# Attention's value matmuls in groups of three key chunks, newest chunk first

## The chip, the cores and the metric

The kernel runs on one core of one Trainium2 chip. The metric is the device time of one execution in microseconds (us); lower is better. Engines are named as in the profile: PE is TensorE's matmul side and PEld its weight loads, DVE is VectorE, ACT is ScalarE, POOL is GpSimd, SP is SyncE, which issues the DMAs.

## The reference

Three parts follow each other: an attention whose queries are pooled by two, and two mixture-of-experts layers on its output.

```python
def _attn_ref(q, k, v):            # each (4, 8, 1152, 64), float32
    B, H, S, D = q.shape
    q_pool = q.reshape(B, H, S // 2, 2, D).mean(axis=3)
    scores = (1.0 / np.sqrt(D)) * np.matmul(q_pool, k.transpose(0, 1, 3, 2))
    scores = scores - np.max(scores, axis=-1, keepdims=True)
    attn = np.exp(scores)
    attn = attn / (np.sum(attn, axis=-1, keepdims=True) + 1e-09)
    return np.matmul(attn, v)

def reference(...):
    x = attention output as (B * 576, H * 64) = (2304, 512)
    x = moe(x, w_gate, w1, w2)     # 8 experts, each takes its best 288 tokens
    return moe2(x, w_skip, w_gate, w1, w2)
```

The change touches the last line of the attention alone. The two expert layers take the second half of the time and are the same before and after.

## The kernel before, in words

Attention works on 16 **pairs**: one batch entry and two neighbouring heads (j = 0, 1). A pair has 9 chunks of 128 keys and two halves of 288 queries (h = 0, 1), so 18 **score steps** (h, c). For one step, `scores` (L213) issues four matmuls on PE: two of 128x128 with 288 columns in float16 (L224, tile `st`), and two of 65x128 (L226), which add the low parts of the split numbers and the negative row maximum. ACT then takes the exponential of both heads at once into a float32 tile `E` (L228), and POOL adds the tile up over the chunks (L233, L235; in the last pair DVE does). `av` (L237) multiplies the chunk's 128 keys of `E` with the values `vt` (L242): one call for each head j, into partitions 0 to 63 or 64 to 127 of the same PSUM tile `av`. A float32 call is two matmuls and two loads in the trace, so a chunk is four matmul rows of 128*64 ("x4"), and one head's half of it is "x2". After the ninth chunk ACT copies `av` out as `o` (L246). `norm` (L249) sums `es` over the partitions with two float32 matmuls of the same 64 columns (L253, tile `ms`), and DVE takes the reciprocal (L256) and multiplies (L257).

While PE works on a pair, it prepares a later one. `scales` (L124 and L129 on ACT and PE, L132 to L145 on DVE) finds power-of-two scales; `split_k` (L151 on ACT, L152 on DVE), `split_q` (L163) and `split_ql` (L167) split into float16 parts; SP transposes them by DMA (L174, L182). `mx` (L193, L196, L197) computes 27 score blocks of 384 keys into the rotating tiles `ms`, whose row maxima DVE reduces (L198); `mxrow` (L205, L207) reduces those nine by nine and transposes them for L226. The pool of `ms` has three buffers, which `mx`, `norm`, `scales`, `tokmajor` (L267, transposes of the finished output) and `logits`/`fold` (L287, L300) share. `st` has two buffers, `E` six, `av` one, `vt` two.

What orders the work: every piece is entered in a plan with a due time in units of score steps (`TA`, `TA0`, `TAL`; a pair is `NSL` = 18 steps) and the plan is emitted sorted by due time. SP keeps the emitted order. For PE, DVE, ACT and POOL a scheduler then goes by emitted order, but passes over what it does not expect to be ready, so the written order is a priority only. Each engine runs its own list strictly in order. The value matmuls of step n are due at n + 3.63:

```python
at(T, (0, 1.0), [lambda i=i, h=h, c=c: scores(i, h, c) for h, c in order])
at(T, (TA["av"], 1.0), [lambda i=i, h=h, c=c: av(i, h, c) for h, c in order])
```

Of the kernel before, what the change touches and what calls it, by code (L numbers as in the profile page):

```python
# [14 lines left out]
P = 128  # L15
NSL = 18
TA = dict(load=-48.62, loadv=-18.39, A=[-35.94, -35.47, -31.75, -29.03, -30.29, -28.09, -23.67], mx=(-19.82, 0.54),
          row=-5.54, av=3.63, norm=[12.26, 21.29], log=[20.27, 23.07, 28.12, 38.2], out=[32.31, 31.08])
TA0 = dict(load=[-94.38, -66.16, -35.31], loadv=[-45.83, -22.29], A=[-76.98, -72.14, -71.71, -68.33, -69.55, -69.2,
          -65.64], mx=(-66.05, 1.19), mx2=(-27.49, 0.55), A1=[-62.02, -58.75, -50.59, -41.02, -44.45, -46.24, -43.53])  # L20
TAL = dict(log=[21.4, 21.59, 24.82, 32.89])
# [26 lines left out]
def attention(tc, q, k, v, w_gate, xd, TL, C, aside=None):  # L48

    nc = tc.nc  # L50
    B, H, S, D = q.shape
    SQ = S // 2
    NP = H // 2
    NC = S // P
# [9 lines left out]
    with ExitStack() as ctx:  # L64
# [12 lines left out]
        E, G = w_gate.shape[1], P // NP  # L77
# [19 lines left out]
        def load(i):  # L97
            b, hp = pairs[i]
            h0 = 2 * hp
            kt = ld.tile([P, 2, NC, D], F32, name="kt")  # L100
            qt = ld.tile([P, NQ, 2, D], F32, name="qt")
            nc.sync.dma_start(kt, k[b, h0:h0 + 2].rearrange("h (p t) d -> p h t d", t=NC))
            nc.sync.dma_start(qt, q[b, h0:h0 + 2].rearrange("h (u r) d -> (h u) r d", r=2)
                              .rearrange("(t p) r d -> p t r d", p=P))
            st[i].update(kt=kt, qt=qt)

        def load_v(i):
            b, hp = pairs[i]
            vt = ldv.tile([P, 2, NC, D], F32, name="vt")
            nc.sync.dma_start(vt, v[b, 2 * hp:2 * hp + 2].rearrange("h (p t) d -> p h t d", t=NC))  # L110
            st[i]["vt"] = vt
# [105 lines left out]
        def scores(i, h, c):  # L217
            s = st[i]
            T1, T2, M1, M2 = s["T1"], T2s[i % 3], s["M1"], s["M2"][:D + 1]
            ps = ps_st.tile([P, 2, 512], F32, name="st")  # L220
            ks = slice(c * P, (c + 1) * P)
            qs = [slice(j * SQ + h * HALF, j * SQ + (h + 1) * HALF) for j in range(2)]
            for j in range(2):
                nc.tensor.matmul(ps[:, j, :HALF], T1[:, j, ks], M1[:, qs[j]], start=True, stop=False)  # L224
            for j in range(2):
                nc.tensor.matmul(ps[:, j, :HALF], T2[:, j, ks], M2[:, qs[j]], start=False, stop=True)  # L226
            e = ep.tile([P, 2, HALF], F32, name="E")
            nc.scalar.activation(e, ps[:, :, :HALF], AF.Exp, scale=s["scl"])  # L228
            s["E", h, c] = e
            add = (nc.vector if i == NPAIR - 1 else nc.gpsimd).tensor_add  # L230
            if c == 1:
                s["es", h] = small.tile([P, 2, HALF], F32, name="es", bufs=2)
                add(s["es", h], s["E", h, 0], e)  # L233
            elif c > 1:
                add(s["es", h], s["es", h], e)  # L235

        def av(i, h, c):  # L237
            s = st[i]
            if c == 0:
                s["av"] = ps_av.tile([P, HALF], F32, name="av")  # L240
            for j in range(2):
                nc.tensor.matmul(s["av"][j * D:(j + 1) * D], s["vt"][:, j, c, :], s["E", h, c][:, j, :],  # L242
                                 start=(c == 0), stop=(c == NC - 1))
            if c == NC - 1:
                s["o", h] = small.tile([P, HALF], F32, name="o", bufs=2)
                nc.scalar.activation(s["o", h], s["av"], AF.Copy)  # L246

        def norm(i, h):
            b, hp = pairs[i]  # L249
            s = st[i]  # L250
            sm = ps_ms.tile([P, HALF], F32, name="ms")
            for j in range(2):
                nc.tensor.matmul(sm[j * D:(j + 1) * D, :], ones64, s["es", h][:, j, :], start=True, stop=True)  # L253
            rs = small.tile([P, HALF], F32, name="rs", bufs=2)
            nc.vector.tensor_scalar_add(rs, sm, 1e-9)
            nc.vector.reciprocal(rs, rs)  # L256
            nc.vector.tensor_mul(xTs[b % 2][:, hp, h * HALF:(h + 1) * HALF], s["o", h], rs)  # L257

        def tokmajor(i, t0, t1):
            b, hp = pairs[i]  # L260
            xT = xTs[b % 2]
            pt = ps_ms.tile([P, 4, P], F32, name="ms")
            n = min(SQ, t1 * P) - t0 * P
            xo = small.tile([P, 4, P], F32, name="xo", bufs=2)
            for t in range(t0, t1):
                m = min(P, SQ - t * P)
                nc.tensor.transpose(pt[0:m, t - t0, :], xT[:, hp, t * P:t * P + m], C["idf"])  # L267
            full = n // P
            if full:
                nc.scalar.activation(xo[:, :full], pt[:, :full], AF.Copy)  # L270
                nc.sync.dma_start(xd[b * SQ + t0 * P:b * SQ + (t0 + full) * P, hp * P:(hp + 1) * P]
                                  .rearrange("(t p) d -> p t d", p=P), xo[:, :full])
            r = n - full * P
            if r:
                nc.scalar.activation(xo[:r, full], pt[:r, full], AF.Copy)
                nc.sync.dma_start(xd[b * SQ + (t0 + full) * P:b * SQ + t0 * P + n, hp * P:(hp + 1) * P], xo[:r, full])
# [33 lines left out]
        def at(t0, ts, fs):  # L310
            ts = [ts[0] + i * ts[1] for i in range(len(fs))] if isinstance(ts, tuple) else ts
            assert len(ts) == len(fs)
            plan.extend((t0 + t, len(plan) + i, f) for i, (t, f) in enumerate(zip(ts, fs)))

        for i in range(NPAIR):
            T = i * NSL
            at(T, [TA["load"] if i > 2 else TA0["load"][i] - T, TA["loadv"] if i > 1 else TA0["loadv"][i] - T],
               [lambda i=i: load(i), lambda i=i: load_v(i)])
            A, B = prep(i)
            at(T, TA0["A"] if i == 0 else TA0["A1"] if i == 1 else TA["A"], A)  # L320
            if i:
                at(T, TA["mx"], B[:-1])
                at(T, [TA["row"]], B[-1:])
            else:
                n0 = 6 * T0 + 1
                at(T, TA0["mx"], B[:n0])
                at(T, TA0["mx2"], B[n0:])
            order = [(h, c) for h in range(2) for c in range(NC)]
            at(T, (0, 1.0), [lambda i=i, h=h, c=c: scores(i, h, c) for h, c in order])
            at(T, (TA["av"], 1.0), [lambda i=i, h=h, c=c: av(i, h, c) for h, c in order])  # L330
            at(T, TA["norm"], [lambda i=i, h=h: norm(i, h) for h in range(2)])
            at(T, TA["out"], [lambda i=i: tokmajor(i, 0, 3), lambda i=i: tokmajor(i, 3, 5)])
            if pairs[i][1] == NP - 1:
                b = pairs[i][0]
                at(T, TAL["log"] if i == NPAIR - 1 else TA["log"],
                   [lambda h=h, f=f, b=b: f(b, h) for h in range(2) for f in (logits, fold)])
# [847 lines left out]
def main(tc, q, k, v, w_gate, w1, w2, w_skip2, w_gate2, w1b, w2b, out):  # L1184
    nc = tc.nc
    n = q.shape[0] * q.shape[2] // 2
    with tc.tile_pool(name="m_one", bufs=1) as one, tc.tile_pool(name="m_dr", bufs=1, space=DRAM) as dr:
        idh = one.tile([P, P], F16, name="idh")
        make_identity(nc, idh)
        idf = one.tile([P, P], F32, name="idf")  # L1190
        make_identity(nc, idf)

        fold = one.tile([P, w_gate.shape[1] + 1], F32, name="fold")
        nc.vector.tensor_reduce(fold, idf.rearrange("p (c s) -> p s c", s=SB)[:, :w_gate.shape[1] + 1], axis=AX.X, op=OP.add)
        C = dict(idh=idh, idf=idf, fold=fold)
        TL = one.tile([P, n // P, w_gate.shape[1]], F32, name="TL")
        xd = dr.tile([n, w_gate.shape[0]], F32, name="xd")
        E = w_gate.shape[1]
        K = {}

        def aside():
            with tc.tile_pool(name="m_tmp", bufs=1) as tmp:
                K.update(moe_setup(tc, one, tmp, dr, w_skip2, w_gate2, E, n))

        attention(tc, q, k, v, w_gate, xd, TL, C, aside)
        moe(tc, xd, TL, w1, w2, w1b, w2b, out, C, K)
# [23 lines left out]
```

## Time and profile before

| | |
|---|---|
| median of 3 runs | 1099.82 us (1096.57 to 1100.39) |
| the profiled execution's own time | 1098.85 us |
| its span, first to last instruction | 1097.0 us, 18678 instructions |
| busy: PE / PEld / DVE / ACT / POOL | 90% / 53% / 70% / 46% / 41% |
| attention | about 0 to 560 us |
| mean granted TensorE clock | 0.950 |

The profile is of one execution. A share of busy time is an average over stages, so the attention has to be read by itself, in stretches. In a timeline of PE a matmul's length reaches past the start of the next one, since matmuls are pipelined; what a matmul costs the engine is the distance from its start to the next start. A bracket behind a row gives the idle time before it and what ended it.

### The profile page before, as it was taken

How to read it: one execution, taken by the hardware profiler on the slowest of the kernel's cores; microseconds unless marked ns; L12 is line 12 of the kernel's file. 1: busy time of each engine (PE TensorE's matmuls, PEld its weight loads, DVE VectorE, ACT ScalarE, POOL GpSimd, SP SyncE). 2: the span in 40 equal slices, each digit the busy share in tenths (PEclk: the TensorE clock that was granted, in tenths of full speed). 3: DMA queues.
4: the chain of work that ended last, by engine and by line, in shares of the span. 5: the costliest groups of instructions: out<-in, count | busy, mean ns of one | idle time of the engine just before them, and what ended most of it. 6: DMA issues, size and time to landing. Idle time of an engine off the chain costs nothing. (4 is left out here: it accounts for less than half of the span.)

```text
span 1097.0 us, 18678 instructions
## 1 busy us (share of the span) xinstructions
PE 989.0 (90%) x6592; PEld 579.9 (53%) x6592; DVE 765.4 (70%) x2107; ACT 507.4 (46%) x874; POOL 450.1 (41%) x361
## 2 busy tenths in 40 slices
PE   3998999999999999999974999999999979888992
PEld 1343344444344444444443777777777756666772
DVE  7887788788888888877567545535546457787751
ACT  3654556565656565654620121211215646867630
POOL 5465667667667667667401013213112122120111
PEclk9899999999999999999975899999999989899996
DMA  6859445435545444531003334333342533757820
GB/s 151 187 140 212 107 116 120 101 67 126 124 114 108 107 82 116 122 74 44 23 23 121 132 99 159 138 99 113 110 173 99 176 120 101 274 141 280 272 73 25
DMA packets 148417, 136.22 MB, mean 124 GB/s; under 512 B 83351, under 2 KB 110999, under 8 KB 148320
## 3 DMA queue, kind: packets, MB, share of 16 engines
q1 hardware_dynamic: 142880, 123.12, 41.0%
q0 software_dynamic: 5440, 11.86, 3.5%
q8 instruction: 54, 0.88, 0.3%
q14 instruction: 43, 0.35, 0.1%
HBM read 94.71 MB, written 21.51 MB: 106 GB/s over the span
## 5 line engine op out<-in xcount | busy, mean ns | idle before, releaser
L235 POOL TENSOR_TENSOR es<-es,E 128x576 f32<-128x576 f32 x210 | 302.8, 1442 | 78.3 <-ACT E L228 70.9
L228 ACT ACTIVATE E<-st,scl 128x576 f32<-128x576 f32 x288 | 212.6, 740 | 205.7 <-PE st L226 184.5
L198 DVE TENSOR_REDUCE nm<-ms 128x1 f32<-128x384 f32 x432 | 228.5, 550 | 80.1 <-PE ms L193 75.6
L242 PE MATMUL av<-E,vt 128*64 128x288 f32 x1152 | 242.8, 430 | 0.0
L193 PE MATMUL ms<-T,M 128*128 128x384 f16 x384 | 124.8, 340 | 22.3 <-DVE nm L198 13.2
L226 PE MATMUL st<-M,T 65*128 65x288 f16 x576 | 126.4, 289 | 0.5 <-DMA M<-QM 0.5
L224 PE MATMUL st<-M,T 128*128 128x288 f16 x576 | 125.0, 292 | 0.6 <-ACT E L228 0.6
L242 PEld LDWEIGHTS av<-E,vt 128*64 128x64 f32 x1152 | 71.1, 135 | 79.7 <-issue 72.6
L842 PE MATMUL mm<-h,raw 128*128 128x288 f32 x384 | 107.8, 421 | 0.0
L814 PE MATMUL mm<-xT,raw 128*128 128x288 f32 x384 | 103.9, 418 | 0.0
L930 POOL DMA_INDIRECT XB<-Y,rowi x24 | 26.2, 1093 | 184.5 <-issue 111.2
L224 PEld LDWEIGHTS <-T 128*128 128x128 f16 x576 | 41.1, 98 | 101.2 <-issue 95.5
L659 POOL DMA_INDIRECT xb<-xd,idi x24 | 24.0, 999 | 159.8 <-DVE ids L656 95.4
L839 PE MATMUL mm<-h,W 128*128 128x288 f16 x576 | 81.9, 300 | 3.1 <-DVE h L819 2.2
L233 POOL TENSOR_TENSOR es<-E 128x576 f32<-128x576 f32 x30 | 43.2, 1440 | 95.9 <-ACT E L228 95.9
L811 PE MATMUL mm<-xT,W 128*128 128x288 f16 x576 | 77.5, 290 | 4.0 <-DVE h L819 4.0
L193 PEld LDWEIGHTS <-M 128*128 128x128 f16 x384 | 37.2, 102 | 82.0 <-issue 69.9
L814 PEld LDWEIGHTS mm<-xT,raw 128*128 128x128 f32 x384 | 69.8, 191 | 18.1
L842 PEld LDWEIGHTS mm<-h,raw 128*128 128x128 f32 x384 | 70.0, 192 | 17.5
L226 PEld LDWEIGHTS <-T 65*128 65x128 f16 x576 | 56.4, 99 | 32.8 <-issue 17.3
L839 PEld LDWEIGHTS <-W 128*128 128x128 f16 x576 | 58.8, 103 | 20.8 <-issue 4.8
L811 PEld LDWEIGHTS <-W 128*128 128x128 f16 x576 | 56.5, 100 | 20.6 <-issue 6.4
(351 smaller groups left out, 1384.4 us busy)
## 6 DMA issues: line engine op xcount, KB each, us to landing
raw<-in_moe_w SPq DMA_DIRECT2D x112, 512.0 KB, 4.4
kt<-in_k SPq DMA_DIRECT2D x16, 576.0 KB
qt<-in_q SPq DMA_DIRECT2D x16, 576.0 KB, 7.3
vt<-in_v SPq DMA_DIRECT2D x16, 576.0 KB, 3.9
XB<-pre SPq DMA_DIRECT2D x3, 1560.0 KB, 20.2
T<-T SPq DMA_DIRECT2D x16, 288.0 KB
xd<-xo SPq DMA_DIRECT2D x16, 192.0 KB
xb<-XB SPq DMA_DIRECT2D x4, 585.0 KB, 14.1
```

Source lines behind the costliest of these rows:

```text
L193: nc.tensor.matmul(pm, M1[:, lo:hi], T1[:, int(lo >= SQ), ks], start=True, stop=True)
L198: nc.vector.tensor_reduce(s["nm"][:, t, i3:i3 + 1], pm, axis=AX.X, op=OP.max)
L224: nc.tensor.matmul(ps[:, j, :HALF], T1[:, j, ks], M1[:, qs[j]], start=True, stop=False)
L226: nc.tensor.matmul(ps[:, j, :HALF], T2[:, j, ks], M2[:, qs[j]], start=False, stop=True)
L228: nc.scalar.activation(e, ps[:, :, :HALF], AF.Exp, scale=s["scl"])
L233: add(s["es", h], s["E", h, 0], e)
L235: add(s["es", h], s["es", h], e)
L242: nc.tensor.matmul(s["av"][j * D:(j + 1) * D], s["vt"][:, j, c, :], s["E", h, c][:, j, :], start=(c == 0), stop=(c == NC - 1))
L811: nc.tensor.matmul(ph, d["W1"][a][:, c, f * P:(f + 1) * P], d["xT"][b][:, c], start=(c == 0 and i == 0), stop=(c == KD - 1 and i == 2))
L814: nc.tensor.matmul(ph, d["R1"][c][:, 0, f * P:(f + 1) * P], d["xT"][:, c], start=(c == 0), stop=(c == KD - 1))
L839: nc.tensor.matmul(py, d["W2"][a][:, f, c * P:(c + 1) * P], d["h"][b][:, f], start=(f == 0 and i == 0), stop=(f == KF - 1 and i == 2))
L842: nc.tensor.matmul(py, d["R2"][f // HK][:, f % HK, c * P:(c + 1) * P], d["h"][:, f], start=(f == 0), stop=(f == KF - 1))
```

## The change

The value matmuls of three neighbouring chunks are now one piece of the plan, due 0.1 steps behind the scores of the third chunk, and inside the piece the third chunk comes first, then the second, then the first. The accumulation's `start` and `stop` flags follow that order. The number of matmuls, their shapes and all other engines' pieces stay.

```diff
-          row=-5.54, av=3.63, norm=[12.26, 21.29], ...
+          row=-5.54, av=0.1, norm=[12.26, 21.29], ...
...
-        def av(i, h, c):
+        def av(i, h, cs):
+
             s = st[i]
-            if c == 0:
+            first, last = cs[-1] == 0, cs[0] == NC - 1
+            if first:
                 s["av"] = ps_av.tile([P, HALF], F32, name="av")
-            for j in range(2):
-                nc.tensor.matmul(s["av"][j * D:(j + 1) * D], s["vt"][:, j, c, :], s["E", h, c][:, j, :],
-                                 start=(c == 0), stop=(c == NC - 1))
-            if c == NC - 1:
+            for c in cs:
+                for j in range(2):
+                    nc.tensor.matmul(s["av"][j * D:(j + 1) * D], s["vt"][:, j, c, :], s["E", h, c][:, j, :],
+                                     start=first and c == cs[0], stop=last and c == cs[-1])
+            if last:
                 s["o", h] = small.tile([P, HALF], F32, name="o", bufs=2)
                 nc.scalar.activation(s["o", h], s["av"], AF.Copy)
...
+            AVS = [(h, list(range(c, min(c + 3, NC)))[::-1]) for h in range(2) for c in range(0, NC, 3)]
             at(T, (0, 1.0), [lambda i=i, h=h, c=c: scores(i, h, c) for h, c in order])
-            at(T, (TA["av"], 1.0), [lambda i=i, h=h, c=c: av(i, h, c) for h, c in order])
+            at(T, [TA["av"] + h * NC + max(cs) for h, cs in AVS], [lambda i=i, h=h, cs=cs: av(i, h, cs) for h, cs in AVS])
```

How the engines' lists move, in a pair of the steady middle part (lines behind `av` are four higher after the change, its own matmul is L245).

PE before, where the scheduler puts single key-maximum matmuls (`ms`) between the two heads' halves of one chunk `E`:

```order
L226 MATMUL st_2947<-M2_2660,T2_1_112 128x288
L242 MATMUL av_2835<-E_2906,vt_2398 64x288
L193 LDWEIGHTS M1_2537
L193 MATMUL ms_2956<-T1_2576,M1_2537 128x384
L242 MATMUL av_2835<-E_2906,vt_2398 64x288
```

PE after, the end of a score step and the group behind it:

```order
L226 MATMUL st_2754<-M2_2667,T2_1_112 128x288
L245 MATMUL av_2635<-E_2735,vt_2061 64x288 x2
L245 MATMUL av_2635<-E_2720,vt_2061 64x288 x2
L245 MATMUL av_2635<-E_2712,vt_2061 64x288 x2
L129 MATMUL ms_2766<-ss_2762,onesf_106 128x2
```

The three chunks stand together, and the score step ahead of them is that of the following chunk: the scheduler let one further score step pass while the third chunk's exponential was expected to run. Over pairs 4 to 13 the list of before has 212 runs of value matmuls, 148 with both halves of one chunk and 64 with one half alone; that of after has 67 runs, 56 with all six calls and 8 with an odd number. Counted together with `norm` and the split maxima (L196, L197), which use 64 columns too, the runs go from 234 to 104.

DVE before, from the end of the scales' chain to the maxima behind the split of the keys:

```order
L141 SCALAR_TENSOR_TENSOR scl<-inv 128x1
L198 TENSOR_REDUCE nm<-ms 128x1
L167 SCALAR_TENSOR_TENSOR QM_110<-qs,S_2764,qh 128x9x64
L198 TENSOR_REDUCE nm<-ms 128x1 x2
L255 TENSOR_SCALAR rs<-ms 128x288
L198 TENSOR_REDUCE nm<-ms 128x1
L256 RECIPROCAL rs<-rs 128x288
L198 TENSOR_REDUCE nm<-ms 128x1
L257 TENSOR_TENSOR xT_121<-o,rs 128x288
L152 SCALAR_TENSOR_TENSOR ks<-kt,S_2764,ks 128x9x64 x2
L198 TENSOR_REDUCE nm<-ms 128x1 x15
```

DVE after, the same place:

```order
L141 SCALAR_TENSOR_TENSOR scl<-inv 128x1
L198 TENSOR_REDUCE nm<-ms 128x1 x3
L258 TENSOR_SCALAR rs<-ms 128x288
L198 TENSOR_REDUCE nm<-ms 128x1
L259 RECIPROCAL rs<-rs 128x288
L198 TENSOR_REDUCE nm<-ms 128x1
L260 TENSOR_TENSOR xT_121<-o,rs 128x288
L152 SCALAR_TENSOR_TENSOR ks<-kt,S_2772,ks 128x9x64 x2
L198 TENSOR_REDUCE nm<-ms 128x1 x5
L167 SCALAR_TENSOR_TENSOR QM_110<-qs,S_2772,qh 128x9x64
L198 TENSOR_REDUCE nm<-ms 128x1 x3
L145 TENSOR_TENSOR qs<-qt 128x576
```

The low part of the queries (L167) has moved behind the split of the keys, and the sum of the next queries (L145) between the later maxima; in the pairs with `logits`, L167 keeps its place. The lists of SP and POOL, and all that belongs to the expert layers, are in the same order as before.

## Rows read from the trace of the kernel before

**Rows 1.** The page: busy time, share of the span and instructions of each engine.

```profile
PE 989.0 (90%) x6592; PEld 579.9 (53%) x6592; DVE 765.4 (70%) x2107; ACT 507.4 (46%) x874; POOL 450.1 (41%) x361
```

**Rows 2.** Busy time by stretch; columns as in its second line.

```profile
core 0: us, PE busy (x) PEld busy (x) DVE busy (x) ACT busy (x) POOL busy (x), PEclk, DMA share, GB/s
30.00:106.56 76.56, 72.39 (x375) 30.14 (x374) 62.05 (x103) 41.34 (x65) 47.15 (x32) 0.96 0.78 182
107.78:114.60 6.82, 6.76 (x18) 2.20 (x17) 4.47 (x13) 4.21 (x6) 2.72 (x2) 0.50 1.05 292
140.78:470.90 330.12, 318.79 (x1964) 139.41 (x1963) 277.36 (x438) 196.99 (x316) 229.76 (x161) 1.00 0.48 108
272.74:305.15 32.41, 31.09 (x192) 13.44 (x191) 27.94 (x44) 19.43 (x31) 22.94 (x17) 1.00 0.49 110
272.74:286.84 14.10, 12.78 (x85) 5.39 (x84) 13.56 (x22) 9.77 (x15) 10.71 (x8) 1.00 0.60 147
```

**Rows 3.** Waits from 140.78 to 470.9: engine, line, releaser, us, times, longest.

```profile
PE ms L193 <- DVE nm L198: 9.2, 7, 1.3
```

**Rows 4.** PE's timeline, a chunk's halves apart: start us, length us, instruction.

```profile
286.84 0.32 PE L193 MATMUL ms<-T,M 128*128 128x384 f16 x1 [1.32 <-DVE nm L198]
...
287.22 0.70 PE L242 MATMUL av<-E,vt 128*64 128x288 f32 x2
287.85 0.50 PE L193 MATMUL ms<-T,M 128*128 128x384 f16 x2
```

**Rows 5.** PE's timeline, two score steps with whole chunks.

```profile
300.54 0.41 PE L226 MATMUL st<-M,T 65*128 65x288 f16 x2
300.88 0.71 PE L242 MATMUL av<-E,vt 128*64 128x288 f32 x4
301.52 0.42 PE L224 MATMUL st<-M,T 128*128 128x288 f16 x2
301.78 0.41 PE L226 MATMUL st<-M,T 65*128 65x288 f16 x2
302.02 0.33 PE L193 MATMUL ms<-T,M 128*128 128x384 f16 x1
302.28 0.71 PE L242 MATMUL av<-E,vt 128*64 128x288 f32 x4
```

**Rows 6.** The last pair's end: loads and matmuls of four chunks in one run.

```profile
555.94 1.65 PEld L242 LDWEIGHTS av<-E,vt 128*64 128x64 f32 x16 [0.24 <-issue]
555.94 2.16 PE L242 MATMUL av<-E,vt 128*64 128x288 f32 x16
...
557.93 0.66 PE L253 MATMUL ms<-es,ones 128*64 128x288 f32 x4
```

**Rows 7.** DVE's timeline in the pair of rows 4.

```profile
276.18 1.36 DVE L167 SCALAR_TENSOR_TENSOR QM<-qs,S,qh 128x576 f16<-128x576 f32 x1
...
297.36 1.69 DVE L145 TENSOR_TENSOR qs<-qt 128x576 f32<-128x576 f32 x1
```

**Rows 8.** ACT's timeline: the exponential behind the score matmuls that start at 301.78.

```profile
302.28 0.74 ACT L228 ACTIVATE E<-st,scl 128x576 f32<-128x576 f32 x1 [0.49 <-PE st L226]
```

**Rows 9.** SP's timeline: issues around the loads of the fourth pair.

```profile
71.34 0.38 SPq L110 DMA_DIRECT2D vt<-in_v  x1
...
72.83 4.73 SPq L399 DMA_DIRECT2D XB<-pre  x3
...
85.00 12.27 SPq L182 DMA_TRANSPOSE M<-qh  x1
```

**Rows 10.** PE's timeline in the last pair.

```profile
540.74 0.42 PE L224 MATMUL st<-M,T 128*128 128x288 f16 x2
...
541.98 0.42 PE L224 MATMUL st<-M,T 128*128 128x288 f16 x2
```

**Rows 11.** PE's timeline ahead of the half-clock stretch of rows 2.

```profile
106.56 0.38 PE L129 MATMUL ms<-ss,onesf 128*128 128x2 f32 x2 [1.70 <-ACT junk L124]
...
107.78 1.01 PE L193 MATMUL ms<-T,M 128*128 128x384 f16 x2 [0.26 <-DVE nm L198]
```

More of the change, by code (lines that the diff above doesn't have):

```diff
@@ L17 @@
 TA = dict(load=-48.62, loadv=-18.39, A=[-35.94, -35.47, -31.75, -29.03, -30.29, -28.09, -23.67], mx=(-19.82, 0.54),
-          row=-5.54, av=3.63, norm=[12.26, 21.29], log=[20.27, 23.07, 28.12, 38.2], out=[32.31, 31.08])
+          row=-5.54, av=0.1, norm=[12.26, 21.29], log=[20.27, 23.07, 28.12, 38.2], out=[32.31, 31.08])
 TA0 = dict(load=[-94.38, -66.16, -35.31], loadv=[-45.83, -22.29], A=[-76.98, -72.14, -71.71, -68.33, -69.55, -69.2,
```

## The prediction

> **What bounds the kernel now.** Start with the shares of the page [rows 1]: PE is busy 90% of the span, DVE 70%. That is a mean over unlike stages, so the next view is busy time by stretch [rows 2]. The stretch from 140.78 to 470.90 holds ten pairs (from one pair's scales matmul, L129, to that ten later), 33.01 us each. Of those PE is busy 31.88 us and DVE 27.74, ACT 19.7, POOL 23.0. The missing 1.13 us of PE are the 11.3 us of the stretch in which it idles; the list of waits [rows 3] puts 9.2 of them on key-maximum matmuls that need an `ms` buffer back from DVE. So PE sets the pace, and DVE stands close behind.
>
> The next cut is inside one pair, 272.74 to 305.15 [rows 2], 32.41 us. **Part A** runs from the scales matmul to the first maximum matmul behind the key splits on DVE, at 286.84 [rows 4]. DVE is busy 13.56 of its 14.10 us, and PE ends it by waiting 1.32. Part A is already DVE's. **Part B** is the other 18.31 us: there DVE is busy 27.94 - 13.56 = 14.38 us only and PE all of it. This cut decides the prediction: what PE saves in part A is worth nothing, what it saves in part B counts.
>
> **What a visit to the 64-column matmuls costs.** Read starts, not lengths [rows 5]. A lone chunk takes 301.52 - 300.88 = 0.64 us until the next score matmul starts. Four chunks in one run take 557.93 - 555.94 = 1.99 us [rows 6], so 0.50 each, with no way out since 64-column matmuls follow. Leaving thus costs 0.64 - 0.50 = 0.14. Entering costs too: from the second pair of score matmuls to a maximum is 302.02 - 301.78 = 0.24, to a value matmul 300.88 - 300.54 = 0.34, so 0.10. A visit costs 0.24 us beside its work. And half a chunk alone takes 287.85 - 287.22 = 0.63 [rows 4]: as much as both halves, which otherwise run side by side, so a lone half wastes 0.25.
>
> [...] Rows 6 show 16 loads beginning with the first matmul and lasting 1.65 us inside the 1.99 of the matmuls: loads do not add to the run. [...]
>
> **PE's work, before and after.** By the lists of the change, over ten pairs the 64-column runs go from 234 to 104 and lone halves from 64 to 8. That is 130 x 0.24 = 31 us and 56 x 0.25 = 14 us, 45 in all, 4.5 us a pair. PE's work falls from 31.88 to 27.4 us, now just under DVE's 27.74. Matmul and load counts do not change, nor any DMA: SP's and POOL's lists keep their order.
>
> **Part A after.** DVE's list here loses L167, 1.36 us [rows 7], which moves behind the splits. The rest stays, so part A should take 14.10 - 1.36 = 12.7 us (12.2 if DVE's gaps vanish too, 13.6 if the longer runs open new ones). PE has in it six score steps of 0.50 (3.0), two groups of 3 x 0.50 + 0.24 = 1.74 (3.5), a norm (0.74), eight maxima of 0.16 (1.3) and three split ones (0.9 as an estimate from the others): 9.4 us. It will wait some 3.3 us in part A, most of it at the same place as before, where the wait grows from 1.32 to about 1.8. Behind it on PE's list stand score steps and maxima, so ACT and DVE get their next tiles later; that is counted in the 12.7.
>
> **Part B after.** PE keeps 27.4 - 9.4 = 18.0 us of work. New waits come on top. The group begins with the newest chunk, whose exponential ends late: the score matmuls of 301.78 end at 302.19, the exponential starts at 302.28 and takes 0.74 [rows 5, 8], so its value matmul can start near 303.1, some 1.2 us after the last score matmul's start. PE has one score step (0.50), the entry and one or two maxima to fill that, so it waits 0 to 0.5 us a group; four groups lie in part B, two of them behind more filler: 0.4. DVE also does L145 (1.69, [rows 7]) ahead of maxima whose buffers PE wants back: 0 to 1. ACT copies `o` only when a group is done, but the exponential behind it needs scores that PE issues after that group anyway: nothing. POOL has 23.0 us of sums for a pair, below any period here, and six `E` buffers stay enough, since at most four chunks wait for a group: nothing; without that cover it would be an exponential's 0.74 per group. I take 18.5 us for part B (18.0 to 19.2).
>
> A pair then takes 12.7 + 18.5 = 31.2 us against 33.01, 1.8 less (0.7 to 2.8 by the bounds). Twelve pairs run like this, the ten and the two behind them: 12 x 1.8 = 21.6 us.
>
> **The other stages.** The first three pairs have even more lone halves, but DVE is busy 62 of the 76.6 us [rows 2], and the fourth pair's transposes wait 12.3 us behind the fill of `XB` [rows 9]. That fill stands on SP's list behind the load of `vt` at 71.34, which needs the first pair's last value matmul; this now comes some 2.5 steps sooner, so the gate moves along. Between nothing and 12 us I take 5, nearer to nothing because of DVE. The last pair makes no new maxima: a step costs 541.98 - 540.74 = 1.24 [rows 10], three cost 3.7. After, three cost 1.5 + 1.74 = 3.2 plus the 0.5 wait for the newest exponential without fillers: nothing gained. From the routing on, all is as before.
>
> **The clock.** In the ten pairs PE's waits of up to 1.32 us leave the granted clock at 1.00 [rows 2, 4]. [...] A fall costs at most 6.82 / 2 = 3.4 us; with one in four of 12 pairs and part of it hidden by DVE's lead I charge 3 us.
>
> **The sum** against the profiled execution's 1098.85 us: minus 21.6, minus 5, plus 3, is 1075 us. The median of the runs is 1099.82, 0.97 above that execution, so on this scale they are the same. A measurement of this kernel can tell about 0.5%, 5.5 us, from no change.
>
> **The rivals.**
> 1. *PE's whole saving arrives.* DVE fills its gaps and a pair falls to its 27.74 us of work plus about 0.8. Twelve pairs save 4.5 each, the start 8: 1037 us. For it, DVE has 5.3 idle us a pair; against it, three `ms` buffers hold too little for DVE to work through a group of 1.74 us and the score step behind it. Chance 0.07.
> 2. *DVE's gaps stay.* Each microsecond that PE wins in part B comes back as a wait for `ms`, because the same maxima now come in bursts between the groups. The pair stays at 33 and only the start gains: 1097 us. For it: part A; against it: DVE's 14.38 of 18.31 in part B. Chance 0.12.
> 3. *Slower, by the clock.* The place is the wait at the end of part A, the price up to 3.4 us of PE's time in each pair, the deciding point a wait somewhere between 1.32 us, which the clock stood, and 1.70, which it did not. If it falls in all 12 pairs: 1098.85 - 21.6 - 5 + 41 = 1113 us. For it, the predicted wait is 1.8; against it, the matmuls right before and behind it are dense, unlike those at 106.56. Chance 0.11.
> 4. [...] Each joined chunk pays its loads, about 1.65 / 4 = 0.4 us a chunk if nothing overlaps. Part B's four groups then pay 8 x 0.4 = 3.2 us, more than the 1.8 saved: 12 x 1.4 = 17 us more and the start's 5 gone, 1116 us. Rows 6 speak against it. Chance 0.02.
>
> That the change does not do what it says is no rival: 56 of 67 runs of value matmuls hold all six calls.
>
> **How the numbers follow.** The forecast has 0.68. Its own range comes from the bounds: 12 x 2.8 + 12 = 46 us gained without a clock fall, 12 x 0.7 = 8 with 6 lost to the clock: 1053 to 1097. Rival 2 is inside, rivals 1, 3 and 4 (0.20) outside. Trimmed at its lower end, where all bounds would have to meet, the range is 1057 to 1097. Faster by over 0.5% means under 1094.3: nearly all of the forecast (0.67), rival 1 (0.07), a little of 2 and 3 (0.03): 0.77. Within 0.5%: most of 2 (0.10), the forecast's edge and mild cases of 3 (0.03): 0.13. Slower: 0.10.
>
> **What would show it.** In the profile after: value matmuls in rows of x12 that start 1.6 to 1.7 us ahead of the next instruction; ten pairs from scales to scales in some 312 us instead of 330; PE's busy share in them lower, DVE's near 89%; PE's waits for DVE's maxima grown from 11 to over 30 us in that stretch, most at the end of part A; short new waits of the value matmuls' loads for `E`. The forecast is wrong if the pair stays at 33 (rival 2), if a joined chunk costs over 0.6 us, or if the granted clock in the middle stretch falls below 0.97.

## The result, and the profile after

| | before | after |
|---|---|---|
| median | 1099.21 us (1096.57 to 1100.39, 4 runs) | 1060.51 us (1058.2 to 1063.14, 4 runs) |
| ratio, 95% interval | | 0.966 (0.9628 to 0.9692) |
| profiled execution and its span | 1098.85, 1097.0 us | 1060.73, 1058.9 us |
| mean granted clock | 0.950 | 0.946 |

The change is 38 us faster. The forecast was 1075 (1057 to 1097), so sign and range hold, and the gain is 14 us larger than forecast. The page's shares hardly tell it: PE goes from 90% [rows 1] to 88%, DVE from 70% to 69%.

```profile
PE 928.8 (88%) x6592; PEld 601.4 (57%) x6592; DVE 733.5 (69%) x2107; ACT 499.9 (47%) x874; POOL 465.9 (44%) x361
```

The view by stretch does tell it. Its rows are the ten pairs, then parts A and B of one pair without `logits` (called a plain pair below), then the stretch up to the end of attention, and the rest.

```profile
core 0: us, PE busy (x) PEld busy (x) DVE busy (x) ACT busy (x) POOL busy (x), PEclk, DMA share, GB/s
135.47:439.30 303.83, 279.65 (x1965) 153.54 (x1963) 255.49 (x437) 192.66 (x316) 243.55 (x161) 1.00 0.52 118
256.97:269.66 12.69, 9.74 (x70) 5.13 (x69) 12.24 (x20) 9.61 (x15) 9.90 (x7) 1.00 0.63 163
269.66:286.93 17.27, 17.17 (x121) 9.65 (x121) 12.91 (x24) 9.51 (x16) 14.67 (x11) 1.00 0.42 87
439.30:520.58 81.28, 76.96 (x538) 42.83 (x536) 59.06 (x98) 45.02 (x73) 48.02 (x33) 1.00 0.21 48
520.58:1058.90 538.32, 467.36 (x3497) 354.00 (x3495) 313.86 (x1377) 191.90 (x376) 90.01 (x94) 0.92 0.41 138
```

The same cuts of before, where they were not yet shown:

```profile
470.91:558.52 87.61, 86.31 (x550) 38.23 (x548) 63.14 (x99) 47.29 (x74) 46.87 (x33) 1.00 0.19 45
558.52:1097.00 538.48, 466.87 (x3497) 353.63 (x3495) 313.50 (x1377) 192.27 (x376) 90.06 (x94) 0.92 0.41 138
```

With [rows 2] the 38.1 us of span split into 140.78 - 135.47 = 5.3 up to the fourth pair, 330.12 - 303.83 = 26.3 in the ten pairs, 87.61 - 81.28 = 6.3 in the last three, and 0.2 in the expert layers.

In the ten pairs PE's work fell from 318.79 to 279.65 us, 3.9 a pair, but the pair by 2.6 only, since PE now waits 24.2 us there instead of 11.3. The plain pair went from 32.41 [rows 2] to 29.96 us: 1.41 of that are in part A (14.10 to 12.69) and 1.04 in part B (18.31 to 17.27). PE's timeline of the plain pair shows both waits of part A and a group on either side of the second:

```profile
261.08 0.71 PE L256 MATMUL ms<-es,ones 128*64 128x288 f32 x4 [1.24 <-DVE nm L198]
261.72 0.34 PE L193 MATMUL ms<-T,M 128*128 128x384 f16 x1
261.98 1.68 PE L245 MATMUL av<-E,vt 128*64 128x288 f32 x12
263.59 0.42 PE L224 MATMUL st<-M,T 128*128 128x288 f16 x2
...
269.66 0.32 PE L193 MATMUL ms<-T,M 128*128 128x384 f16 x1 [1.71 <-DVE nm L198]
```

A group of three costs 263.59 - 261.98 = 1.61 us. In the list of waits of the ten pairs (as in [rows 3]) PE's waits for DVE's maxima are 14.7 + 6.9 = 21.6 us, and the loads' new waits for `E` are many and short:

```profile
PEld av L245 <- ACT E L228: 15.3, 50, 0.4
PE ms L193 <- DVE nm L198: 14.7, 12, 1.7
...
PE ms L256 <- DVE nm L198: 6.9, 8, 1.2
```

What keeps PE waiting is in DVE's timeline of part A, where one 128x1 operation takes 1.13 us:

```profile
259.33 1.13 DVE L141 SCALAR_TENSOR_TENSOR scl<-inv 128x1 f32<-128x1 f32 x1
260.39 1.48 DVE L198 TENSOR_REDUCE nm<-ms 128x1 f32<-128x384 f32 x3
...
265.30 3.84 DVE L152 SCALAR_TENSOR_TENSOR ks<-kt,S,ks 128x576 f16<-128x576 f32 x2
```

POOL's timeline has a sum that starts before it and ends with it, at 260.45, and another that starts just before the key splits (L152):

```profile
259.05 1.40 POOL L233 TENSOR_TENSOR es<-E 128x576 f32<-128x576 f32 x1 [0.72 <-ACT E L228]
...
265.18 1.47 POOL L235 TENSOR_TENSOR es<-es,E 128x576 f32<-128x576 f32 x1 [1.14 <-ACT E L228]
```

In all ten pairs of before the 128x1 operation (L141) took 0.15 us, in the pairs of after 1.13 to 1.27. The view by source line, before and then after (duration in ns as min/median/max):

```profile
L141 DVE SCALAR_TENSOR_TENSOR scl<-inv x10: 148/149/151, 143.3 to 439.3; 128x1 f32<-128x1 f32 x10
```

```profile
L141 DVE SCALAR_TENSOR_TENSOR scl<-inv x9: 1132/1144/1265, 167.8 to 410.4; 128x1 f32<-128x1 f32 x9
```

The theory to be tested is therefore: (1) the gain is PE's saved visits to the 64-column matmuls; (2) in part A PE's saving reaches the end only as far as DVE's list lets it; (3) DVE's list is stretched by POOL's sums beside it. The main rivals are that the earlier due time or DVE's new order brings the gain, and that DVE's durations are its own.

### The profile page after: what moved, and what is told of

It is laid out like the page before. It is cut to its first block, busy times and chain, and to the rows that moved or that the text cites. A ratio compares the mean times of both kernels' runs of the same rounds, so it can differ in the third digit from the quotient of the medians.

```text
span 1058.9 us, 18491 instructions
## 1 busy us (share of the span) xinstructions
PE 928.8 (88%) x6592; PEld 601.4 (57%) x6592; DVE 733.5 (69%) x2107; ACT 499.9 (47%) x874; POOL 465.9 (44%) x361
## 5 line engine op out<-in xcount | busy, mean ns | idle before, releaser
L235 POOL TENSOR_TENSOR es<-es,E 128x576 f32<-128x576 f32 x210 | 319.3, 1521 | 61.6 <-ACT E L228 49.5
L228 ACT ACTIVATE E<-st,scl 128x576 f32<-128x576 f32 x288 | 207.3, 738 | 143.2 <-PE st L226 139.1
L198 DVE TENSOR_REDUCE nm<-ms 128x1 f32<-128x384 f32 x432 | 218.9, 545 | 56.8 <-PE ms L193 54.2
L245 PE MATMUL av<-E,vt 128*64 128x288 f32 x1152 | 171.5, 418 | 3.7 <-ACT E L228 2.6
L193 PE MATMUL ms<-T,M 128*128 128x384 f16 x384 | 116.2, 340 | 32.3 <-DVE nm L198 20.3
L226 PE MATMUL st<-M,T 65*128 65x288 f16 x576 | 124.0, 289 | 1.6 <-DMA M<-QM 1.6
L245 PEld LDWEIGHTS av<-E,vt 128*64 128x64 f32 x1152 | 77.3, 137 | 69.9 <-ACT E L228 27.3
L934 POOL DMA_INDIRECT XB<-Y,rowi x24 | 26.3, 1094 | 184.1 <-issue 111.0
L224 PEld LDWEIGHTS <-T 128*128 128x128 f16 x576 | 49.7, 98 | 72.3 <-issue 56.7
L233 POOL TENSOR_TENSOR es<-E 128x576 f32<-128x576 f32 x30 | 42.5, 1417 | 58.6 <-ACT E L228 58.6
```

Of the source, the lines that this page charges most:

```text
L193: nc.tensor.matmul(pm, M1[:, lo:hi], T1[:, int(lo >= SQ), ks], start=True, stop=True)
L198: nc.vector.tensor_reduce(s["nm"][:, t, i3:i3 + 1], pm, axis=AX.X, op=OP.max)
```

## The experiments

All times are in us, and each edit is against the change unless said otherwise. The runs of before beside them had medians of 1098.67 (the first four), 1096.54 (the next four) and 1098.79 (the last four).

**Groups of one.**

```diff
-            AVS = [(h, list(range(c, min(c + 3, NC)))[::-1]) for h in range(2) for c in range(0, NC, 3)]
+            AVS = [(h, list(range(c, min(c + 1, NC)))[::-1]) for h in range(2) for c in range(0, NC, 1)]
```

> The changed kernel with its new due time (0.1) but groups of one chunk. By the lists, ten pairs then have 211 runs of 64-column matmuls and 38 lone halves, where the change has 104 and 8. Theory of visits (0.24 us for each run, 0.25 us for each lone half): 10.7 x 0.24 + 3 x 0.25 = 3.3 us of PE more in a pair, of which the waits at the end of part A hide about a third: +2.2 us a pair, 12 pairs, about 1087 us (1078 to 1095). Rival, the earlier due time alone brings the gain: about 1061 us as the change.

Measured 1100.34, ratio 1.0009 (0.998 to 1.0037): no gain at all, so the due time alone brings nothing. Ten pairs:

```profile
143.72:471.83 328.11, 317.51 (x1965) 143.61 (x1963) 255.08 (x437) 194.69 (x317) 232.43 (x161) 1.00 0.47 109
```

PE's work is back at 31.75 a pair; the pair is 2.4 longer than in the change where 2.2 was expected. My total was short because the 8.3 lost before the fourth pair (143.72 against 135.47) were not in it, and of the 8.5 in the last three (to the last value matmul at 560.79, in the change at 519.76) only two pairs of 2.2. DVE's list went back with PE's: L167 stands ahead of the key splits again (147.2 and 153.4), so this run takes the joining and DVE's new order away together. Its order alone is edited below (L167 back ahead of the key splits).

**Oldest chunk first.**

```diff
-            AVS = [(h, list(range(c, min(c + 3, NC)))[::-1]) ...
+            AVS = [(h, list(range(c, min(c + 3, NC)))) ...
```

> Groups of three as in the change, but the oldest chunk first. The lists then show 131 runs and 24 lone halves in ten pairs instead of 104 and 8, since norms and split maxima fall elsewhere. Theory of visits: 2.7 x 0.24 + 1.6 x 0.25 = 1.05 us of PE more in a pair, two thirds of it on the path: about 1069 us (1064 to 1073). Rival, the newest chunk's exponential is what the groups wait for (15.3 us of load waits for E in ten pairs): with the oldest first these waits go and the time falls to 1050 us or less. A second rival, the order inside a group means nothing: 1061 us.

Measured 1069.09, ratio 0.9727 (0.9671 to 0.9783). The number is the expected one, the way to it is not. First the ten pairs, then one plain pair:

```profile
134.19:445.40 311.21, 295.18 (x1964) 149.60 (x1963) 261.04 (x438) 195.48 (x316) 238.07 (x160) 0.98 0.52 115
226.46:256.17 29.71, 28.18 (x191) 14.60 (x190) 25.56 (x44) 19.39 (x31) 23.85 (x16) 1.00 0.58 120
```

PE is busy 1.55 longer a pair, but part of that is time at a granted clock of 0.50 (mean of the ten pairs 0.98); in the plain pair, all of it at 1.00, PE has 28.18 - 26.91 = 1.27 more work. Even so the plain pair is not longer, since PE's waits hide it. The 7.4 us come in other pairs: the one from 256.17 took 31.21 at a mean clock of 0.95, with 3.41 us at 0.50 from 269.14 on. The loads' waits for `E` went only from 15.3 to 12.1, so the rival of the newest exponential falls.

**Heads apart in a group.**

```diff
-            for c in cs:
-                for j in range(2):
+            for j in range(2):
+                for c in cs:
```

> As the change, except that a group issues its chunks for head 0 and then its chunks for head 1, so that the two heads' 64-column matmuls no longer alternate. Runs are as long and as many as in the change, every other instruction stands where it stood. If the two halves run side by side only when they alternate (a lone half took as long as both), a full group takes 6 x 0.5 + 0.24 = 3.2 us instead of 1.74: +1.5 us for each of 6 groups, 9 us of PE a pair, less some 2 us of PE's idle time: about 1061 + 12 x 7 = 1145 us (1110 to 1165). Rival, only the length of a run counts: 1061 us.

Measured 1108.74, ratio 1.0094 (1.0066 to 1.0122). Against the change that is 48 us worse, with runs of the same length, so length alone is not it; but the price was overestimated. PE's timeline, the two groups of a part A:

```profile
280.70 2.21 PE L245 MATMUL av<-E,vt 128*64 128x288 f32 x12
282.85 0.42 PE L224 MATMUL st<-M,T 128*128 128x288 f16 x2
...
285.53 2.21 PE L245 MATMUL av<-E,vt 128*64 128x288 f32 x12
288.92 0.32 PE L193 MATMUL ms<-T,M 128*128 128x384 f16 x1 [1.18 <-DVE nm L198]
```

A group takes 282.85 - 280.70 = 2.15 instead of 1.61, so 6 x 0.54 = 3.2 a pair, not 9. Nearly all of it arrives: ten pairs take 334.38, 3.06 more each. Part A grew by 0.54 of the 1.08 added there although PE waits in it: DVE stood idle 0.39 more there, at a maximum behind the first longer run, and L141 took 1.28 instead of 1.13.

**L167 back ahead of the key splits.**

```diff
-A=[-35.94, -35.47, -31.75, -29.03, -30.29, -28.09, -23.67]
+A=[-35.94, -35.47, -31.75, -33.0, -30.29, -28.09, -23.67]
```

> The change with one due time moved (fourth of the list A from -29.03 to -33.0), which puts DVE's L167 ahead of the key splits again, as it stood before the change; PE's groups stay. Theory that PE's shorter list brings the gain: part A grows by what L167 takes there, 0.8 to 1.36 us, part B shrinks by some of it: 1066 to 1074 us. Rival, the gain is DVE's new order (L167 out of part A, DVE's two-input operations no longer beside POOL's sums): 1085 us or more, with L145 and L167 back at 1.69 and 1.36 us.

Measured 1081.23, ratio 0.9827 (0.9766 to 0.9888): between the two, worse than my theory said. The ten pairs, parts A and B of a plain pair, and 3.41 us of another pair:

```profile
137.22:456.06 318.84, 285.66 (x1964) 159.32 (x1962) 265.12 (x437) 192.91 (x316) 239.03 (x161) 0.98 0.48 112
263.46:277.78 14.32, 10.41 (x74) 6.09 (x73) 13.87 (x21) 10.21 (x16) 11.71 (x8) 1.00 0.56 145
277.78:294.41 16.63, 16.54 (x117) 9.34 (x116) 12.54 (x23) 8.90 (x15) 12.25 (x10) 1.00 0.44 90
341.34:344.75 3.41, 3.41 (x12) 1.61 (x11) 2.46 (x5) 1.25 (x2) 2.02 (x2) 0.50 0.90 168
```

Part A grows by 1.63, as L167 takes 1.77 there (0.80 in part B), and part B gives back 0.64. On top comes the clock, in PE's timeline at the end of part A in two pairs:

```profile
277.78 0.32 PE L193 MATMUL ms<-T,M 128*128 128x384 f16 x1 [2.14 <-DVE nm L198]
```

```profile
341.34 0.48 PE L193 MATMUL ms<-T,M 128*128 128x384 f16 x1 [2.06 <-DVE nm L198]
```

The second wait was followed by 3.41 us at 0.50, the first was not. The pair of the second took 33.12 at a mean clock of 0.95, that of the first 30.95 at 1.00; over the ten pairs the mean is 0.98. Moving L167 back thus takes 20.7 of the 38 us away and leaves 17.4, so both rivals hold in part: PE's shorter list does not bring the whole gain, and DVE's new order does not either. The plain pair parts them. With L167 back, part A takes 14.32, no less than the 14.10 of before, and part B 16.63 against 18.31: all that PE's shorter list saves there lies in part B, as the prediction's cut said, and part A's gain goes with the place of L167. How far the clock adds to the 20.7 is an estimate: the mean granted clock is 0.941 over this run's 1078.6 us of span and 0.946 over the change's 1058.9, so 63.6 and 57.2 us of full speed are missing and the clock adds about 6 us at most. The kernel before with L167 moved and nothing joined was not run; the next runs bound it.

**POOL's sums left out**, in the change and in before (in `scores`):

```diff
-            elif c > 1:
+            elif c > 1 and i == NPAIR - 1:
                 add(s["es", h], s["es", h], e)
```

> The change with GpSimd's running sums of the exponentials left out beyond the second chunk (all pairs but the last), so the denominators are short and GpSimd does one add of 128x576 instead of eight for each half of the queries. Theory that DVE's operations with two SBUF inputs are stretched by GpSimd's sums beside them: L152 falls from 1.92 us to about 0.8 in every pair, L141 from 1.13 to 0.15, L145 stays 0.74; part A loses 2 x 1.1 + 1.0 = 3.2 us of DVE, its waits of 2.95 us of PE nearly vanish, the pair falls from 30.4 to about 27.5 us and the run to about 1030 us. Rival, these durations are DVE's own (form, operands, stride): they stay, and the time stays at 1061 us.

> The kernel before with the same sums left out. There PE sets the pace (31.88 of 33.01 us a pair), so shorter operations of DVE can only take away the 1.13 us in which PE waits: 32.0 us a pair, about 1087 us. Against the run of the change without the sums this is the price of the visits alone, with DVE out of the way: 4.5 us a pair by the prediction. Rival, DVE's stretched operations are what bounds the kernel before too: under 31 us a pair.

Measured 1039.96, ratio 0.9483 (0.9456 to 0.951), and 1080.05, ratio 0.9849 (0.9822 to 0.9876). Ten pairs, of the change and of before:

```profile
133.96:424.39 290.43, 278.19 (x1965) 152.48 (x1963) 231.76 (x437) 191.67 (x316) 28.06 (x20) 1.00 0.53 123
```

```profile
138.49:456.05 317.56, 317.56 (x1965) 139.42 (x1964) 236.29 (x438) 196.97 (x316) 28.07 (x20) 1.00 0.49 113
```

In before PE is busy in all of the 317.56: with DVE out of the way PE's list is the time, 31.76 a pair. So as long as PE's list stays, nothing done to DVE's list, its order included, can bring a pair of before under 31.76, and the change's takes 30.38. The change does the same work in 27.82 of PE. DVE's busy time fell by 24 and 41 us with no operation of its own changed, and L152 fell from a mean of 1.72 in the change to 0.81:

```profile
L152 DVE SCALAR_TENSOR_TENSOR ks<-kt,S,ks 128x576 f16<-128x576 f32 x20 | 15.6, 811 | 0.0
L141 DVE SCALAR_TENSOR_TENSOR scl<-inv 128x1 f32<-128x1 f32 x9 | 12.1, 1345 | 0.0
```

L141, expected at 0.15, stayed at 1.35; the only sums that POOL still does are those of the second chunk (L233), and in the change it is one of these that runs beside L141. The pair came to 29.0 and not to the expected 27.5.

**L141 in another form.**

```diff
-nc.vector.scalar_tensor_tensor(scl, invf[:, 0:1], QSCALE, invf[:, 1:2], op0=OP.mult, op1=OP.mult)
+nc.vector.tensor_scalar(scl, invf[:, 0:1], invf[:, 1:2], QSCALE, op0=OP.mult, op1=OP.mult)
```

> The change with one small operation of DVE written differently: the scale factor (L141, 128x1) as a tensor_scalar with one tensor input and a pointer scalar instead of a scalar_tensor_tensor with two tensor inputs. If an operation with two tensor inputs in SBUF must wait for GpSimd's sum to end, its 1.13 us fall to 0.15 and everything behind it in part A comes 1.0 us sooner: pair -0.5 to -1.0, 12 pairs, 1049 to 1055 us. Rival, the 1 us is a wait of that place for something else (or part A is not bound by DVE's list): no change, 1061 us.

Measured 1037.65, ratio 0.9458 (0.9434 to 0.9481): 23 us for one operation of 128x1, at least twice what was expected. DVE's timeline, POOL's sum behind the key splits, and ten pairs:

```profile
249.83 0.20 DVE L141 TENSOR_SCALAR scl<-inv 128x1 f32<-128x1 f32 x1
...
254.86 1.54 DVE L152 SCALAR_TENSOR_TENSOR ks<-kt,S,ks 128x576 f16<-128x576 f32 x2
```

```profile
255.65 2.02 POOL L235 TENSOR_TENSOR es<-es,E 128x576 f32<-128x576 f32 x1 [1.13 <-ACT E L228]
```

```profile
132.44:420.56 288.12, 279.65 (x1964) 153.21 (x1962) 235.34 (x437) 191.30 (x316) 239.63 (x161) 1.00 0.54 124
```

POOL's sum of 249.55 ran for 1.41 us, so the new form takes 0.20 in the middle of it. What comes behind starts 0.94 sooner, counted from the pair's scales matmul, and thereby the key splits begin 0.79 us before POOL's next sum (255.65) instead of just behind it: 1.54 for both instead of 3.84. The plain pair is 27.57, PE's work in it 26.91. In the ten pairs none of the splits waits in three pairs and one of the two in seven; in the change both wait in seven and one in three.

**The two key splits as one operation.**

```diff
-                    nc.vector.scalar_tensor_tensor(ks[:, j, :, 1, :], kt[:, j], s["S"][:, 0:1], ks[:, j, :, 0, :], ...
+                nc.vector.scalar_tensor_tensor(ks2[:, :, 1, :], kt2, s["S"][:, 0:1], ks2[:, :, 0, :], ...
```

> The change with the two key splits on DVE (L152, 128x576 each, 3.84 us together) done as one operation of 128x1152 behind both of ACT's halves. If each such operation has to wait for GpSimd once, one operation waits once: about 2.7 us instead of 3.84, part A -1.1 us, 12 pairs, about 1049 us (1046 to 1055), unless it begins later because ACT's second half ends later (0.77 us, then about 1059). [...]

Measured 1046.82, ratio 0.9531 (0.9493 to 0.9568): as expected, 2.56 us instead of 3.84, one wait instead of two.

```profile
L153 DVE SCALAR_TENSOR_TENSOR ks<-kt,S,ks x11: 2555/2567/2569, 142.0 to 439.9; 128x1152 f16<-128x1152 f32 x11
```

**The new form of L141 in before.** The same edit there.

> The kernel before with only the scale factor (L141) written with one tensor input. Theory that PE's visits set the pace there: without GpSimd's sums, which took every stretched operation off DVE, PE was busy in all of the 31.76 us of a pair, so no shortening of DVE's list can bring a pair of before under that; the most to be had is 33.01 - 31.76 = 1.25 us a pair, 15 us in all, and one operation less of 1 us will bring 5 to 13: 1085 to 1094 us (the same edit took 23 us off the change). Rival, the edit is worth the same in both kernels: 1076 us.

Measured 1100.11, ratio 1.0007 (0.9986 to 1.0029): worth nothing. My 5 to 13 us were wrong for a plain reason: in before L141 took 0.15 already (the source line's row above), so there was nothing to shorten.

**Both edits of DVE's list**, L141's form and the one key split.

> The change with both edits of DVE's list, the scale factor with one tensor input and the two key splits as one operation. With the first edit alone a plain pair took 27.57 us, of which PE was busy 26.91, and the splits already found GpSimd idle (0.77 us each). Theory that PE is the bound again: nothing more to be had there, about 1036 us (1033 to 1041). Rival, the two gains add up (-23 and -14): about 1024 us.

Measured 1039.14, ratio 0.946 (0.9427 to 0.9494): no better than the first alone, as expected if PE is the bound again: it is busy 279.85 of the 286.97 us of the ten pairs.

**L141's form with groups of four, and of two.** In the line of groups, `c + 4` and `c + 2` with the same step.

> The change with the scale factor's edit and groups of four chunks instead of three. By the lists, 83 runs in ten pairs instead of 104, lone halves 8 as before: 2.1 x 0.24 = 0.5 us of PE less in a pair; as PE is the bound now, 12 x 0.5 = 6 us: 1032 us. Rival, runs of 2.1 us instead of 1.6 leave ACT and DVE without work, as the longer runs of the heads apart did (+0.53 us of run became +0.54 us of part A): 1040 to 1050 us.

> The change with the scale factor's edit and groups of two chunks. By the lists, 130 runs and 26 lone halves in ten pairs instead of 104 and 8: 2.6 x 0.24 + 1.8 x 0.25 = 1.07 us of PE more in a pair, and with PE the bound all of it on the path: 12 to 14 pairs, 1051 to 1053 us. Rival, shorter runs feed DVE more evenly, so that it waits less and the loss is smaller: 1037 to 1043 us.

Measured 1083.84, ratio 0.9834 (0.979 to 0.9878), and 1104.12, ratio 1.0042 (1.0025 to 1.0058), against 1037.65 with groups of three: all four expectations were far too low. Of groups of four, DVE's row by source line and ten pairs:

```profile
L136 DVE TENSOR_SCALAR S<-se x10: 153/1298/1315, 138.3 to 428.2; 128x2 int32<-128x2 int32 x10
```

```profile
136.18:458.70 322.52, 290.64 (x1964) 162.15 (x1963) 267.79 (x437) 192.11 (x317) 234.20 (x161) 0.96 0.47 111
```

L136, 0.15 in the ten pairs of the change, now stands beside a sum of POOL, at 268.37 beside the one that starts at 268.24, and delays the scales; and the clock's mean is 0.96 over the ten pairs. With groups of two it is 0.95, after waits such as the 2.25 at 290.56:

```profile
290.90:294.31 3.41, 3.41 (x9) 1.01 (x9) 1.55 (x4) 0.00 (x0) 1.79 (x2) 0.50 0.92 173
```

The counts of visits cannot be read from these two runs. The mean granted clock is 0.932 over a span of 1083.0 us with groups of four, 0.934 over 1107.1 with groups of two and 0.947 over 1038.2 with groups of three: 73.6, 73.1 and 55.0 us of full speed are missing, so the clock can account for at most 19 and 18 us as an estimate. How much of the rest of the 46 and 66 us is DVE's stretched operations and how much the other places of `norm` was not taken apart.

## Why the prediction was right, and where its sizes were off

| term | forecast | measured |
|---|---|---|
| up to the fourth pair | -5 | -5.3 |
| ten pairs | -18 (10 x 1.8) | -26.3 |
| last three pairs | -3.6 (2 x 1.8, then 0) | -6.3 |
| clock, in the ten pairs | +3 | 0 |
| rest | 0 | -0.2 |

**PE's work** was forecast to fall by 4.5 a pair to 27.4 and fell by 3.9, to 27.97. The two runs without sums give the same, 31.76 to 27.82. The group's price held: 1.74 was forecast with 0.10 for entering, and the 1.61 from its own start make 1.71 with it. Counted from start to start over the ten pairs, the value matmuls fell by 33.8 us where 130 x 0.14 for leaving and 14 for the halves make 32.2; all other matmuls, which pay the entries, fell by 5.2 where 130 x 0.10 = 13 was forecast. So it is the entries that were priced too high; why is open. Groups of one, with the change's due time and none of its joining, gave back all of the gain, with PE's work back at 31.75: what PE saves is the visits.

**Part A** was forecast at 12.7 with a wait of about 1.8 at its end and some 3.3 in all; it took 12.69, with 1.71 and 1.24. It came out so well by luck, since deviations of both signs nearly cancelled: L167 left as said, and L260, 1.06 on average as L257 before, took 0.45; but L141 took 1.13 where it had taken 0.15. PE's work in it was 9.74 and not 9.4. The reason given, that part A is DVE's list, is shown by the two edits of that list alone: 14 us for the joined split, 23 us for L141.

**Part B is the step that failed.** "PE keeps 27.4 - 9.4 = 18.0 us of work", then 0.4 of waits, "I take 18.5": it took 17.27, with 17.17 of work and 0.10 of waits. The 27.4 came from the mean over ten pairs (31.88), which holds the pairs with `logits`, while part A's 9.4 and both lengths were cut from a plain pair, whose work was 31.09 [rows 2]. That is 0.8 too much. And no group waited in part B: the loads' waits for `E` are 0.3 on average and lie under matmuls still running. Ten times these 1.23 us are 12.3; the mean pair (30.38) is 0.42 longer than a plain one (29.96), which takes 4.2 back; 8.1 remain, and that is the difference between 26.3 and the forecast's 18.1 in the ten pairs. The same mixing made the 1.8 a pair: a plain 31.2 was set against the mean 33.01. Against the plain 32.41 it is 1.2, all of it from part A, where 2.45 were measured. The lower bound of the 1.8 was also added up wrongly: 33.01 - 13.6 - 19.2 is 0.2 and not 0.7, which put the upper end of the range 6 us too low; the result is far from that end.

**The start** was right by luck. The gate that was to move did not. SP issued the load of `vt` and the fill of `XB` 0.3 and 0.2 us sooner than in [rows 9], and the transpose behind them left SP's list 0.4 later, at 97.64:

```profile
71.03 0.38 SPq L110 DMA_DIRECT2D vt<-in_v  x1
...
72.60 4.05 SPq L403 DMA_DIRECT2D XB<-pre  x3
...
86.91 10.73 SPq L182 DMA_TRANSPOSE M<-qh  x1
```

Of the 5.3 us, 2.8 lie between the last two scales matmuls ahead of the ten pairs (106.56 to 140.78 before, 104.05 to 135.47 after), a saving like that of the ten, and 2.5 ahead of them.

**The last pairs** saved 6.3 and not 3.6. From norm to norm, the last two took 46.4 together against 49.2, the one ahead of them 30.0 against 32.3, and the remaining 1.3 belong to the end of one more pair, which the count of two left out.

**The clock** was charged 3 us and cost nothing in the ten pairs: a wait of 1.71 a pair left 1.00 over them. One fall of 3.4 us in every fourth of 12 pairs was the author's estimate from the 6.82 us at 0.50 of [rows 2], and no run shows it: the change's ten pairs have no fall, and those read in a pair of other runs lasted 3.41 us at 0.50, 1.7 us of full speed. Ahead of the ten pairs the change has 17.07 us at 0.50 from 26.03 on where before has 10.24 from 25.87 on; what that costs is inside the 5.3. Falls of the clock as in rival 3 came in the oldest-first, the L167 and the other group sizes' runs (means of 0.98, 0.98, 0.96 and 0.95 over their ten pairs). Its deciding point, a wait between 1.32 and 1.70, is refuted by 1.71 here, by 2.14 and 2.06 in one kernel, one without a fall and one with, and by a fall at 269.14 in the oldest-first run, right behind waits of 0.70 and 0.58. What decides a fall was not shown.

**The other rivals.** Rival 2 (DVE's gaps stay, 1097) did not happen. Rival 1 (PE's whole saving, 1037) did not happen in the change, but the new form of L141 gave just that, 1037.65, with the same three `ms` buffers: what stood against it was not their number, as I argued, but one operation of DVE beside a sum of POOL. Rival 4 (each joined chunk pays its loads) falls: the loads of one group in PE's weight-load timeline last 1.17 us inside the 1.61:

```profile
281.56 1.17 PEld L245 LDWEIGHTS av<-E,vt 128*64 128x64 f32 x12 [0.42 <-ACT E L228]
```

Of what the profile was to show, x12 rows 1.61 ahead of the next instruction are there and the short waits for `E` too. The ten pairs took 304 and not 312; PE waits for DVE's maxima 21.6 us and not over 30; DVE's share is 255.49 / 303.83 = 84% and not 89%, since L145, L167 and L260 became cheaper where they now run, which was not foreseen.

## What to carry to other kernels

Price a change of order at the engine that sets the pace in each stage, and take every duration in one sum from the same kind of iteration: a mean over unlike ones put 0.8 us too much into each pair here. When the bound moves to an engine with a helper beside it, look for the short operations whose time is far above their size, since they can be waits in disguise: one 128x1 operation in another form was worth 23 of 1060 us here, and nothing in the kernel before. A better count of visits alone is no forecast either: with L141's new form, groups of four have 83 runs by the lists instead of 104 and were 46 us slower than groups of three, in a run where other operations met POOL's sums and the clock fell.

## What the runs showed of the hardware that was not expected

**DVE waits for POOL.** Two operations of DVE with two operands in SBUF, L152 and L141, took 0.81 us (mean, without the later sums) and 0.15 (ten of ten in before, as at 275.27 ahead of the sum at 275.51) where POOL was idle. Where L141 started behind a running sum of POOL, it ended with that sum, within 0.02 us in nine of nine in the change, and took 1.13 to 1.27, without the later sums up to 1.35; L152, started at 265.30, took 1.96 and ended 0.6 us behind the sum's end at 266.65. Two such operations in a row waited twice (3.84 against 2.56 joined). Started first, they did not wait: two in 1.54, ahead of POOL's sum, and then the sum was the longer one, 2.02 instead of 1.40. The int32 tensor_scalar of 128x2 (L136) went from 0.15 to 1.30 in the same way, the 128x1 tensor_scalar with a pointer scalar (L141's new form) did not: 0.196 to 0.200 in ten of ten, also at 249.83, 277.64 and 308.50, inside sums that started at 249.55, 277.12 and 308.33. Maxima, which read PSUM, took 0.49 to 0.56 inside a sum and outside. Why some operations waited and others did not was not shown.

**Side-by-side halves.** Twelve 64-column matmuls that alternated between the two heads' halves of `av` took 1.61 us in the change, the same twelve with each head's six together 2.15.
